# Slot numbers of two or three routed tiles in one set of matmuls, and one query load moved, in an attention, MoE and FFN kernel

## The chip, the cores and the metric

The kernel runs on one core of a Trainium2 chip. The metric is the device time of one execution in microseconds (us); lower is better. Engines are named as in the profile: PE (TensorE matmuls), PEld (its weight loads, which overlap PE), DVE (VectorE), ACT (ScalarE), POOL (GpSimd), SP (the engine that issues most DMAs; SPq is its queue).

## The reference, cut to what matters

```python
# 1. attention, 2 batches x 8 heads, 512 local + 32 global queries, head 64
s_g = scale * q_g @ k_all.T                      # global queries see all keys
s_l = concat([scale * q_l @ k_g.T, where(|i - j| <= 32, scale * q_l @ k_l.T, -1e9)])
out = concat([softmax(s_g) @ v_all, softmax(s_l) @ v_all])
x = out as [1152 tokens, 512]
# 2. top-1 routing to 8 experts with a capacity
expert_idx = argmax(x @ w_gate)
for i in range(N):                               # tokens in order
    e = expert_idx[i]
    if counts[e] < capacity:
        disp[e, counts[e]] = x[i]; pos[i] = counts[e]; counts[e] += 1; keep[i] = True
h = maximum(einsum('ecd,edf->ecf', disp, w1), 0); y = einsum('ecf,efd->ecd', h, w2)
out[i] = gate_w[i] * y[expert_idx[i], pos[i]] if keep[i] else 0
# 3. FFN: x @ w_in, a piecewise activation, @ w_out
```

The change touches the numbers `pos[i]` of part 2, the load of `q_g` in part 1, and matmuls that compute nothing at the kernel's start.

## The kernel before

**Attention** is a loop over 16 steps k = (batch b, half tp of the local queries, pair hp of heads). A unit u = 4 b + hp holds the keys, queries and values of one pair of heads in one batch. Step k issues, in this order on every engine: the exponentials of step k + 1 (`exps`, ACT), the scores of step k + 2 (`scores`: L308 on PE, L313 on DVE), the list `first[k]`, the transposes of step k (`transp`, L333), their copies (`evac_t`, L338 on ACT and L339 on DVE), the product with the values of step k - 1 (`av`, L351 on PE, copy L356 on DVE), and the list `plan[k]`. There is no scheduler: each engine runs its instructions in the order in which the code issues them, and semaphores keep them apart.

**Global queries** are treated in four groups g of two units, by `glob1` (products L367 on PE, maxima L372 to L375 on DVE), `glob1b` (exponentials L383 and L385 on ACT, then L388, L390 and L391 on DVE), `glob2` and `glob3` (L419 on PE, L424 on ACT). They lie in `plan` from steps 0, 3, 5 and 8 on; `glob1` of the last group (g = 3) is in step 8. Its queries, the tile `qgt` for units 6 and 7, are loaded by `load_values(7)`, which is in `plan[6]`, as the last of the DMAs of unit 7. All the loads of this stage (keys and queries `kr` and `qr`, L124 and L125; values `vt`, L130; `qgt`, L133; expert weights `raw`, L205; zeros that fill the routing buffer `xd`, L621) are issued by SP in program order.

**Routing** is done in four parts of tiles of tokens (a tile is 128 tokens, the tile of global tokens 32): (b, lo, hi) = (0, 0, 3), (0, 3, 5), (1, 0, 3) and (1, 3, 5). For each part, `recips` (L507, L508), `logits`, `choose` (up to L536, which writes the one-hot expert of each token, `OH`), `slots` (the running number of each token within its expert, `sidx`), `x_rows` (L487 on PE, L501 on DVE or L498 on ACT) and `scatter` (L566, an indirect DMA that POOL issues). `slots` is in steps 8, 11 and 14, and after the loop for the last part. It makes, tile by tile, a sum of small matmuls in PSUM: the base row of each expert (L547), the counts of all earlier parts (`racc`, L548), the one-hot tiles of the same part that come earlier (L550) and the tokens before each one in its own tile (`tri_b`, L551); so 3, 4 and 5 matmuls for three tiles, 3 and 4 for two. DVE then multiplies with `OH`, reduces to `sidx` and adds to `racc` (L554 to L561).

In steps 5 to 12 a chunk of expert weights is rounded on ACT (`weight_h`, L218) and the rest is taken on POOL (`weight_l`, L230), each at the end of its step and so behind the step's `scatter` on POOL.

After the loop, the last part's rows are brought by a matmul with a matrix of ones (`place`, L739) straight into the first expert's input, and then come the eight experts (L842, L860) and the FFN (L1158, L1198).

**At the start** `keep_warm(WARM_0)` runs nine matmuls of zeros of 512 columns (L629), each with a load of 128 weight columns, ahead of the first `scores`. There are further such bursts around the last `slots`.

Of the kernel before, what the change touches and what calls it, by code (L numbers as in the profile page):

```python
# [8 lines left out]
F32 = mybir.dt.float32  # L9
F32R = mybir.dt.float32r  # L10
BF16 = mybir.dt.bfloat16
# [5 lines left out]
ENG = mybir.EngineType  # L17

P = 128
WARM_0, WARM_1, WARM_2, WARM_3, WARM_4 = 9, 5, 3, 2, 0  # L20
WIN = 224


# [5 lines left out]
def tile_attention_moe_ffn(  # L29
# [23 lines left out]
    nc = tc.nc  # L53
    w_in, w_out = w_in.bitcast(U32), w_out.bitcast(U32)
    B, NHP = qd.shape[0], qd.shape[1]
    SL = qd.shape[3]
    EXT = kd.shape[3]
    SG = qg.shape[3] // 4
# [3 lines left out]
    E, _, F = w1.shape  # L62
# [14 lines left out]
    at = actx.enter_context(tc.tile_pool(name="at", bufs=1))  # L77
# [19 lines left out]
    def ps_a(name):  # L97
        return ps_tile("A", name)
# [4 lines left out]
    def ps_v(name, hold=False):  # L103
        return ps_tile("V", name, hold)
# [7 lines left out]
    KR, QR, VT, QG = {}, {}, {}, {}  # L112

    def load_unit(u, part=None):
        b, hp = divmod(u, NHP)
        if part in (None, 0):
            KR[u] = at.tile([P, EXT], F32, tag="kr", name=f"kr{u}", bufs=NBU)
            QR[u] = at.tile([P, SL], F32, tag="qr", name=f"qr{u}", bufs=NBU)

        for i, (k0, k1, q0, q1) in enumerate(((0, SL // 2 + 96, 0, SL // 2), (SL // 2 + 96, EXT, SL // 2, SL))):  # L120
            if part in (None, i) and (part is not None or i == 0):
                if part is None:
                    k1, q1 = EXT, SL
                nc.sync.dma_start(KR[u][:, k0:k1], kd[b, hp, :, k0:k1])  # L124
                (nc.scalar if u == 0 else nc.sync).dma_start(QR[u][:, q0:q1], qd[b, hp, :, q0:q1])  # L125

    def load_values(u):
        b, hp = divmod(u, NHP)
        VT[u] = at.tile([P, 5, P], F32, tag="vt", name=f"vt{u}", bufs=NBU)
        nc.sync.dma_start(VT[u], vx[b, hp])  # L130
        if hp % 2 == 1:
            QG[u // 2] = at.tile([P, 4 * SG], F32, tag="qgt", name=f"qgt{u}", bufs=4)
            nc.sync.dma_start(QG[u // 2], qg[b, hp // 2])  # L133

    mask_sb = at.tile([P, NLT, WIN], F32, name="mask_sb")
    load_unit(0, 0)
# [4 lines left out]
    zero = const.tile([P, DM], F32, name="zero")  # L141
    nc.gpsimd.memset(zero, 0.0)
    ident = const.tile([P, P], F32, name="ident")
    make_identity(nc, ident)
    load_values(0)
    load_unit(3, 0)
    load_values(1)
    for u in range(NHP):
        load_unit(u, 1)
    nc.sync.dma_start(mask_sb[:, 2:], masks[:, 2:])  # L150
    load_values(2)
    load_values(3)
    wg_sb = const.tile([P, NHP, 32], F32, name="wg_sb")
# [7 lines left out]
    tri_b = const.tile([P, P], BF16, name="tri_b")  # L161
    ones_b = const.tile([P, P], BF16, name="ones_b")
    half = const.tile([P, 1], F32, name="half")
    racc = const.tile([P, E], BF16, name="racc")
    base_b = const.tile([P, E], BF16, name="base_b")
# [131 lines left out]
    def scores(s):  # L297
        b, tp, hp = steps[s]
        u = b * NHP + hp
        SM[s] = at.tile([P, 4, WIN], F32, tag="sm", name=f"sm{s}", bufs=4)  # L300
        NG[s] = at.tile([P, 4], F32, tag="ng", name=f"ng{s}", bufs=3)

        sp = [{1: ps_t, 2: ps_v}.get(s, ps_a)(f"sp{s}_{h}") for h in range(2)]
        for t in range(2):
            i = 2 * tp + t
            for h in range(2):
                hs = slice(D * h, D * h + D)
                nc.tensor.matmul(sp[h][:, t * WIN:(t + 1) * WIN], QR[u][hs, i * P:(i + 1) * P],  # L308
                                 KR[u][hs, i * P:i * P + WIN], start=True, stop=True)
        for h in range(2):  # L310
            for t in range(2):
                c = 2 * t + h
                nc.vector.tensor_tensor_reduce(  # L313
                    out=SM[s][:, c, :], in0=sp[h][:, t * WIN:(t + 1) * WIN], in1=mask_sb[:, 2 * tp + t, :],
                    op0=ALU.add, op1=ALU.min, scale=-scale, scalar=3.0e38, accum_out=NG[s][:, c:c + 1])
# [113 lines left out]
    LG, M8, I8, OH, SC, PL, XR = {}, {}, {}, {}, {}, {}, {}  # L429
# [10 lines left out]
    def tile_rows(i):  # L440
        return SG if i == 0 else P
# [98 lines left out]
    def slots(b, lo, hi):  # L540

        pc = ps_v(f"pc{b}{lo}")
        n = hi - lo
        for i in range(lo, hi):
            o = pc[:, E * (i - lo):E * (i - lo + 1)]
            r = tile_rows(i)
            nc.tensor.matmul(o, ones_b[:1], base_b[:1], start=True, stop=False)  # L547
            nc.tensor.matmul(o, ones_b, racc, start=False, stop=False)  # L548
            for j in range(lo, i):
                nc.tensor.matmul(o, ones_b[:tile_rows(j)], OH[b][:tile_rows(j), j, :], start=False, stop=False)  # L550
            nc.tensor.matmul(o, tri_b[:r], OH[b][:r, i, :], start=False, stop=True)  # L551
        ts = slice(b * NB_ + lo, b * NB_ + hi)
        ex = rt.tile([P, NB_, E], F32, tag="ex", name=f"ex{b}{lo}", bufs=1)
        nc.vector.tensor_tensor(  # L554
            out=ex[:, :n, :], in0=pc[:, :E * n].rearrange("p (i e) -> p i e", e=E), in1=OH[b][:, lo:hi, :],
            op=ALU.mult)
        rs = rt.tile([P, E], F32, tag="rs", name=f"rs{b}{lo}", bufs=1)
        nc.vector.tensor_reduce(out=rs, in_=OH[b][:, lo:hi, :].rearrange("p i e -> p e i"), op=ALU.add, axis=AX.X)
        with nc.allow_low_precision(reason="whole numbers, one of the terms not zero"):
            nc.vector.tensor_reduce(out=sidx[:, ts], in_=ex[:, :n, :], op=ALU.add, axis=AX.X)  # L560
        nc.vector.tensor_tensor(out=racc, in0=racc, in1=rs, op=ALU.add)  # L561
# [61 lines left out]
            nc.sync.dma_start(yd[0:1, :], zero[:1, :])  # L623


    def keep_warm(n):
        warm = ps_a("warm")
        for _ in range(n):
            nc.tensor.matmul(warm, zero.bitcast(BF16)[:, :P], zero.bitcast(BF16)[:, :512], start=True, stop=True)  # L629

    keep_warm(WARM_0)
    scores(0)
    exps(0)
    scores(1)
# [6 lines left out]
    load_values(4)  # L641
    load_unit(5)
    load_values(5)
    wq = [(u, c) for u in range(2) for c in range(4)]
    wn = 0

# [12 lines left out]
    def route(k, b, tp):  # L659

        lo, hi = (0, 3) if tp == 0 else (3, 5)
        i = 2 * tp + 1
        x = [lambda j=j: x_rows(b, j) for j in range(lo, hi)]
        sc = [lambda j=j: scatter(b, j) for j in range(lo, hi)]
        first[k] += [lambda: logits(b, i, 2), lambda: recips(b, i, i + 2)]
        plan[k] += [lambda: logits_t(b, i, 2)]
        if tp == 0:
            first[k].append(lambda: logits(b, 0, 1))
            plan[k].append(lambda: logits_t(b, 0, 1))
        plan[k] += [lambda: choose(b, lo, hi)]  # L670
        first[k + 1] += x[:1]
        plan[k + 1] += [lambda: slots(b, lo, hi)] + x[1:2] + sc[:1]
        plan[k + 2] += x[2:] + sc[1:]
# [42 lines left out]
    for i in (3, 4):  # L716
        x_rows(1, i, (2, 3))
    keep_warm(WARM_1)
    slots(1, 3, NB_)
    late = [XR[1, 3], XR[1, 4]]  # L720
    halves = [[rt.tile([P, DM], F32R, name=f"late{i}{n}") for n in "hl"] for i in range(2)]
# [6 lines left out]
    for (xa, xb), x in zip(halves, late):  # L728
        nc.vector.tensor_tensor(out=xb, in0=x, in1=xa.bitcast(F32), op=ALU.subtract)
    px0 = ps_t("px0")  # L730
    keep_warm(WARM_2)
    parts = [(halves[i][0], place[:, i, :]) for i in range(2)] + [(xt0, ident)]
    parts += [(halves[i][1], place[:, i, :]) for i in range(2)]
# [14 lines left out]
    pc = ps_v("pcnt")  # L748
# [662 lines left out]
```

## Time and profile before

| | |
|---|---|
| runs | 462.73, 465.33, 465.10 us; median 465.1 us |
| the profiled execution | 462.71 us, of which the span from first to last instruction is 460.8 us |
| PE, PEld busy | 442.3 us (96% of the span), 372.1 us (81%) |
| DVE, ACT, POOL busy | 335.2 us (73%), 242.9 us (53%), 95.8 us (21%) |
| instructions | 8110, of them 2875 matmuls |

Each engine's busy share is a mean over stages with different limits: attention with routing ends some 91 us after the span's start, the experts at 254 us, the FFN at the end. What ends the waits within a stage is read from the order of time there, in which each line has its start, its length, the engine, the line of code, and in brackets how long the engine was idle before it and what released it.

### The profile page before, as it was taken

Reading aid. Unit: us, or ns where it says so; the run is one execution under the profiler, and the core shown is the slowest. Engines: PE = TensorE matmul, PEld = TensorE weight load, DVE = VectorE, ACT = ScalarE, POOL = GpSimd, SP = SyncE. Lnnn points to the kernel's source line nnn. Section 1 sums busy time; section 2 is a strip of 40 time slices with the busy share of each in tenths; the row PEclk is TensorE's granted clock in tenths of the full one; section 3 lists DMA queues with packets and bytes.
Section 4 is the critical chain, followed back from the end, with each engine's and each line's share of the span. In section 5 each row is a group of like instructions: output and inputs, shape, how many; then the busy total and the mean of one; then the engine's idle time right before and its main releaser. Section 6 shows DMA issues by size and latency. Waiting matters only on the chain. (4 is left out here: it accounts for less than half of the span.)

```text
span 460.8 us, 8110 instructions
## 1 busy us (share of the span) xinstructions
PE 442.3 (96%) x2875; PEld 372.1 (81%) x2876; DVE 335.2 (73%) x715; ACT 242.9 (53%) x508; POOL 95.8 (21%) x98
## 2 busy tenths in 40 slices
PE   8998989999999999999999899998999999999997
PEld 4876677787577777777777799998999899999996
DVE  4787798674156389936898976787888988878633
ACT  5779666273244478726766675645444344534321
POOL 1105365300000000000001642232133131322321
PEclk9999999999999999999999999999999999999999
DMA  8999554589349169963986340653221410000203
GB/s 273 312 332 366 171 185 134 192 278 395 129 127 316 47 242 389 375 239 123 341 299 243 98 149 0 211 200 93 91 75 64 134 49 1 0 2 0 70 1 127
DMA packets 34595, 79.17 MB, mean 172 GB/s; under 512 B 3761, under 2 KB 8497, under 8 KB 34546
## 3 DMA queue, kind: packets, MB, share of 16 engines
q1 hardware_dynamic: 31698, 70.40, 44.8%
q0 software_dynamic: 1408, 4.46, 2.9%
q10 hardware_dynamic: 1440, 3.67, 2.3%
q8 instruction: 29, 0.48, 0.5%
q14 instruction: 20, 0.16, 0.1%
HBM read 63.77 MB, written 14.75 MB: 170 GB/s over the span
## 5 line engine op out<-in xcount | busy, mean ns | idle before, releaser
L1158 PE MATMUL fh<-oldH,H 128*128 128x256 f32 (+1 forms) x256 | 64.7, 328 | 2.6 <-DVE g L1176 2.1
L230 DVE TENSOR_TENSOR L<-raw,H 128x1024 fp32r<-128x1024 f32 x56 | 66.3, 1217 | 0.9 <-ACT H L218 0.6
L1198 PE MATMUL acc<-oldH,H 128*128 128x256 f32 (+2 forms) x240 | 65.1, 332 | 1.3 <-ACT H L280 0.7
L218 ACT CAST H<-raw 128x1024 fp32r<-128x1024 f32 x57 | 58.0, 1049 | 10.0 <-PEq L895 8.2
L1158 PEld LDWEIGHTS fh<-oldH,H 128*128 128x128 f32 x256 | 44.8, 189 | 6.0 <-DVE g L1176 2.5
L1184 ACT CAST oldH<-g 128x256 fp32r<-128x256 f32 (+2 forms) x36 | 17.9, 496 | 56.8 <-DVE g L1176 56.8
L1198 PE MATMUL acc<-oldH,L 128*128 128x256 f32 (+2 forms) x144 | 47.2, 328 | 0.0
L1198 PEld LDWEIGHTS acc<-oldH,H 128*128 128x128 f32 x240 | 43.3, 189 | 4.0 <-issue 1.0
L1172 DVE SCALAR_TENSOR_TENSOR r<-r 128x256 f32<-128x256 f32 (+2 forms) x48 | 31.2, 650 | 21.0 <-ACT r L1163 21.0
L1185 POOL TENSOR_TENSOR oldH<-g,oldH 128x256 fp32r<-128x256 f32 (+2 forms) x24 | 26.8, 1119 | 73.3 <-ACT oldH L1184 63.5
L1158 PE MATMUL fh<-oldH,L 128*128 128x448 f32 (+1 forms) x128 | 41.6, 325 | 0.0
L599 DVE TENSOR_TENSOR hl<-pt,hh 128x512 fp32r<-128x512 f32 (+1 forms) x24 | 15.7, 653 | 35.6 <-ACT hh L598 35.6
L860 PE MATMUL py<-H,hh 128*128 128x512 f32 (+1 forms) x96 | 38.6, 402 | 0.0
L860 PE MATMUL py<-L,hh 128*128 128x512 f32 (+1 forms) x96 | 37.6, 391 | 0.0
L285 DVE TENSOR_TENSOR L<-co,H 128x512 fp32r<-128x512 f32 x32 | 22.9, 722 | 18.4 <-ACT H L280 18.4
L1163 ACT ACTIVATE r<-fh,half 128x256 f32<-128x256 f32 (+2 forms) x48 | 27.0, 564 | 17.5 <-PE fh L1158 17.1
L845 ACT ACTIVATE hs<-ph 128x512 f32<-128x512 f32 (+1 forms) x24 | 14.4, 598 | 41.2 <-PE ph L842 41.0
L1158 PE MATMUL fh<-oldL,H 128*128 128x384 f32 x128 | 35.2, 339 | 0.2
L931 POOL DMA_INDIRECT yg_own<-yd,idx x2 | 2.3, 1135 | 147.5 <-DVE co L270 147.2
L270 DVE SCALAR_TENSOR_TENSOR co<-raw,ca 128x512 uint32<-128x512 uint32 x32 | 31.5, 992 | 0.9
L324 ACT ACTIVATE sm<-sm,ng 128x224 f32<-128x224 f32 x64 | 30.0, 476 | 3.7 <-DVE ng L313 3.7
L860 PE MATMUL py<-H,hl 128*128 128x512 f32 (+1 forms) x96 | 28.5, 401 | 0.0
(202 smaller groups left out, 1014.8 us busy)
## 6 DMA issues: line engine op xcount, KB each, us to landing
raw<-in_w_dram SPq DMA_DIRECT2D x64, 512.0 KB, 5.7
raw<-in_w_in_dram SPq DMA_DIRECT2D x14, 512.0 KB, 4.9
raw<-in_w_out_dram SPq DMA_DIRECT2D x12, 512.0 KB, 3.7
xd<-zero SPq DMA_DIRECT2D x16, 256.0 KB, 5.9
vt<-in_vx_dram SPq DMA_DIRECT2D x8, 320.0 KB, 4.8
xt<-xd SPq DMA_DIRECT2D x8, 256.0 KB, 6.5
yd<-zero SPq DMA_DIRECT2D x8, 256.0 KB, 3.7
yd<-ys SPq DMA_DIRECT2D x8, 256.0 KB, 5.6
```

What stands on the lines that cost most here:

```text
L218: nc.scalar.copy(dst, src)
L230: eng.tensor_tensor(out=L[:, sl], in0=RAW.pop((u, c)), in1=H[:, sl].bitcast(F32), op=ALU.subtract)
L270: nc.vector.scalar_tensor_tensor(out=o, in0=lo, scalar=29, in1=a, op0=ALU.logical_shift_right, op1=ALU.bitwise_or)
L285: nc.vector.tensor_tensor(out=L[:, sl], in0=CV.pop((g, c)), in1=H[:, sl].bitcast(F32), op=ALU.subtract)
L324: nc.scalar.activation(SM[s][:, c, :], SM[s][:, c, :], AF.Exp, bias=NG[s][:, c:c + 1], scale=-1.0, accum_out=SUM[b][:, i, col:col + 1])
L860: nc.tensor.matmul(py[:rows], h[:, 4 * q + k, :rows], w[:, 4 * q + k, :], start=q == i == 0, stop=q == 1 and i == len(terms) - 1)
L1158: nc.tensor.matmul(ph[:, :n], w[:, k, :], XC[c][i // 2][:, k, :], start=n_ == 0, stop=n_ == len(terms) - 1)
L1163: nc.scalar.activation(RS[f % 2][:, :n], ph[:, :n], AF.Relu, bias=half, scale=0.5)
L1172: nc.vector.scalar_tensor_tensor(out=r[:, :n], in0=r[:, :n], scalar=1.0, in1=r[:, :n], op0=ALU.min, op1=ALU.mult)
L1184: nc.scalar.copy(gh[:, :n], gt[:, :n])
L1185: nc.gpsimd.tensor_tensor(out=gl[:, :n], in0=gt[:, :n], in1=gh[:, :n].bitcast(F32), op=ALU.subtract)
L1198: nc.tensor.matmul(a[:, :n], p[:, ds], q, start=f == 0 and i == 0, stop=f == nfl - 1 and i == 2)
```

## The change

1. `slots` writes the slot numbers of all tiles of a part into one row of PSUM: one matmul each for the base row and for `racc`, with the moving operand repeated over the tiles, one matmul for each earlier tile that adds it to all later tiles at once, and one with `tri_b` for all tiles. Three tiles take 5 matmuls in place of 12, two take 4 in place of 7. The tile of global tokens is now read over all 128 rows.
2. `load_queries` is split off `load_values`, and the queries of group 3 are loaded right behind `load_values(5)`, ahead of the loop, and no longer behind the values of unit 7.
3. The burst at the start has 29 matmuls of 160 columns in place of 9 of 512.

```diff
-WARM_0, WARM_1, WARM_2, WARM_3, WARM_4 = 9, 5, 3, 2, 0
+WARM_0, WARM_1, WARM_2, WARM_3, WARM_4 = 29, 5, 3, 2, 0
...
-        if hp % 2 == 1:
-            QG[u // 2] = at.tile([P, 4 * SG], F32, tag="qgt", name=f"qgt{u}", bufs=4)
-            nc.sync.dma_start(QG[u // 2], qg[b, hp // 2])
+        if hp % 2 == 1 and u // 2 not in QG:
+            load_queries(u // 2)
+
+    def load_queries(g):
+        QG[g] = at.tile([P, 4 * SG], F32, tag="qgt", name=f"qgt{g}", bufs=4)
+        nc.sync.dma_start(QG[g], qg[divmod(2 * g, NHP)[0], 2 * g % NHP // 2])
...
-        for i in range(lo, hi):
-            o = pc[:, E * (i - lo):E * (i - lo + 1)]
-            r = tile_rows(i)
-            nc.tensor.matmul(o, ones_b[:1], base_b[:1], start=True, stop=False)
-            nc.tensor.matmul(o, ones_b, racc, start=False, stop=False)
-            for j in range(lo, i):
-                nc.tensor.matmul(o, ones_b[:tile_rows(j)], OH[b][:tile_rows(j), j, :], start=False, stop=False)
-            nc.tensor.matmul(o, tri_b[:r], OH[b][:r, i, :], start=False, stop=True)
+        o = pc[:, :E * n].rearrange("p (i e) -> p i e", e=E)
+        nc.tensor.matmul(o, ones_b[:1], base_b[:1].unsqueeze(1).to_broadcast([1, n, E]), start=True, stop=False)
+        nc.tensor.matmul(o, ones_b, racc.unsqueeze(1).to_broadcast([P, n, E]), start=False, stop=False)
+
+        for j in range(1, n):
+            nc.tensor.matmul(o[:, j:], ones_b, OH[b][:, lo + j - 1:lo + j, :].to_broadcast([P, n - j, E]),
+                             start=False, stop=False)
+        nc.tensor.matmul(o, tri_b, OH[b][:, lo:hi, :], start=False, stop=True)
...
-    def keep_warm(n):
+    def keep_warm(n, cols=512):
         warm = ps_a("warm")
         for _ in range(n):
-            nc.tensor.matmul(warm, zero.bitcast(BF16)[:, :P], zero.bitcast(BF16)[:, :512], start=True, stop=True)
-
-    keep_warm(WARM_0)
+            nc.tensor.matmul(warm[:, :cols], zero.bitcast(BF16)[:, :P], zero.bitcast(BF16)[:, :cols], start=True,
+                             stop=True)
+
+
+    keep_warm(WARM_0, 160)
...
     load_unit(5)
     load_values(5)
+    load_queries(3)
```

## Rows read from the trace of the kernel before

**Rows 1.** Busy time by stage: stretch, length, busy time of each engine, clock, DMA share.

```profile
76.90:84.70 7.80, 7.74 (x85) 6.77 (x82) 5.73 (x18) 0.59 (x1) 2.84 (x3) 1.00 0.28 101
91.30:254.00 162.70, 159.41 (x755) 120.98 (x756) 109.96 (x166) 93.90 (x145) 3.26 (x4) 1.00 0.71 253
254.00:460.80 206.80, 198.82 (x1180) 187.85 (x1180) 157.31 (x277) 91.36 (x177) 60.90 (x56) 1.00 0.24 76
```

**Rows 2.** PE in order of time, step 8: start, length, work, idle time and releaser.

```profile
42.90 1.03 PE L308 MATMUL sp<-kr,qr 64*128 64x224 f32 x8 [1.88 <-DVE m L532]
...
46.21 1.67 PE L419 MATMUL gpv<-gT,vt 128*64 128x32 f32 x40
...
48.82 1.12 PE L367 MATMUL g<-kr,qgt 64*32 64x288 f32 x16 [0.94 <-DMA qgt<-in_qg_dram]
...
49.87 0.17 PE L547 MATMUL pc<-base_b,ones_b 1*128 1x8 bf16 x1
...
50.94 0.64 PE L487 MATMUL px<-ident,xT 128*128 128x128 f32 x4
```

**Rows 3.** The line that loads keys, 41.0 to 42.0 us (unit 7): issue and landing.

```profile
L124 SPq DMA_DIRECT2D kr<-in_kd_dram x1: 422/422/422, 41.6 to 41.6; - x1
...
DMA to landing us min/median/max: 5.4/5.4/5.4
```

**Rows 4.** The line that loads local queries, 36.0 to 36.2 us (unit 6): issue and landing.

```profile
L125 SPq DMA_DIRECT2D qr<-in_qd_dram x1: 733/733/733, 36.0 to 36.0; - x1
...
DMA to landing us min/median/max: 6.7/6.7/6.7
```

**Rows 5.** SP's queue where the moved load goes (the queries of group 2).

```profile
20.95 0.43 SPq L133 DMA_DIRECT2D qgt<-in_qg_dram  x1
```

**Rows 6.** Busy time, clock, DMA share and GB/s ahead of step 8.

```profile
33.00:43.00 10.00, 8.04 (x120) 6.35 (x118) 7.45 (x31) 9.90 (x32) 5.30 (x3) 1.00 1.02 377
```

**Rows 7.** DVE and POOL in order of time, steps 8 and 9.

```profile
49.56 0.46 DVE L372 TENSOR_REDUCE gs<-g 128x1 f32<-128x288 f32 x1 [2.57 <-PE g L367]
...
51.12 0.18 DVE L554 TENSOR_TENSOR ex<-pc,oh 128x24 f32<-128x24 f32 x1 [0.32 <-PE pc L551]
...
52.40 1.11 POOL L566 DMA_INDIRECT xd<-xr,sidx  x1 [7.62 <-DVE xr L501]
...
53.55 2.37 POOL L230 TENSOR_TENSOR L<-raw,H 128x1024 fp32r<-128x1024 f32 x1
...
54.98 0.97 DVE L388 SCALAR_TENSOR_TENSOR gs<-gs 128x1 f32<-128x1 f32 x1
```

**Rows 8.** DVE and POOL in order of time, steps 10 to 13.

```profile
58.45 2.53 DVE L507 TENSOR_SCALAR ssum<-ssum 128x16 f32<-128x16 f32 x1
...
58.57 4.78 POOL L230 TENSOR_TENSOR L<-raw,H 128x1024 fp32r<-128x1024 f32 x2
...
67.47 0.99 POOL L566 DMA_INDIRECT xd<-xr,sidx  x1 [4.11 <-DVE racc L561]
...
72.05 2.39 POOL L230 TENSOR_TENSOR L<-raw,H 128x1024 fp32r<-128x1024 f32 x1
```

**Rows 9.** PE and DVE in order of time, the slots of step 11.

```profile
66.19 0.17 PE L547 MATMUL pc<-base_b,ones_b 1*128 1x8 bf16 x1
...
66.81 0.17 DVE L554 TENSOR_TENSOR ex<-pc,oh 128x16 f32<-128x16 f32 x1 [0.25 <-PE pc L551]
```

**Rows 10.** PE in order of time, the slots of step 14.

```profile
76.97 0.17 PE L547 MATMUL pc<-base_b,ones_b 1*128 1x8 bf16 x1
...
78.16 0.64 PE L487 MATMUL px<-ident,xT 128*128 128x128 f32 x4
```

**Rows 11.** DVE in order of time, the last slots.

```profile
86.89 0.16 DVE L554 TENSOR_TENSOR ex<-pc,oh 128x16 f32<-128x16 f32 x1
```

**Rows 12.** PE in order of time, the start.

```profile
1.31 3.88 PE L629 MATMUL warm<-zero 128*128 128x512 bf16 x9 [1.31 <-POOL zero L142]
...
5.12 1.91 PE L308 MATMUL sp<-kr,qr 64*128 64x224 f32 x16
```

## The prediction

> **What bounds the kernel now.** I read the stages first [rows 1]: in the experts and in the FFN PE is busy for 159.41 of 162.70 us and 198.82 of 206.80 us. None of the change's instructions run there. Time that the change gains or loses ahead of the experts should therefore arrive at the end almost unchanged, as their start and the weight loads that follow freed buffers move with it. The question is only what the change does to the first 91 us, and there I read the order of time, engine by engine, around `slots`, around the moved load and at the start. The reader is to see three kinds of bound in turn. Up to step 8 the bound is the DMA queue: its engines are fully booked from 33 to 43 us [rows 6], and PE, which idles for 1.88 us ahead of the scores at 42.90, starts just after unit 6's queries land at 36.0 + 6.7 = 42.7 us [rows 2, 4]. (The row names a DVE instruction as releaser; by its own line that had long been needed for nothing in `scores`, whose operands are `qr` and `kr`.) From there to the slots of step 8 PE itself is the chain, except for one hole: it ends `glob3` at 46.21 + 1.67 = 47.88 and starts `glob1` of group 3 at 48.82, held for 0.94 us by its queries [rows 2]. From step 9 to 13 the chain goes through DVE and POOL: POOL takes up scatters when DVE's rows are ready, then rounds weights, and DVE instructions wait for the end of that [rows 7, 8]. Last, from 76.90 to 84.70 it is PE again, busy for 7.74 of 7.80 us [rows 1].
>
> **The moved load: what it gives.** With `qgt` there since some 20 us earlier, the 0.94 us go, if nothing else is late. Next in line are the keys of unit 7: 41.6 + 5.4 = 47.0 us, 0.9 us before PE is through with `glob3` [rows 2, 3]. So the whole 0.94 us is free to go. DVE has 2.57 us idle ahead of the maxima of group 3 [rows 7], so it follows PE.
>
> **The moved load: what it costs.** It is 128 rows of 128 floats, 65.5 KB, on SP's queue at about 21.4 us, behind the load of group 2 [rows 5]; it is moved past the zero fills of `xd`, the first expert weights and the loads of units 6 and 7, which are all behind it now. In a queue that moves 377 GB/s at full share [rows 6] it is worth 65.5 / 377 = 0.17 us; as an issue on SP it is 0.43 us [rows 5]. The landing at 42.7 us that PE waits for [rows 4] moves by that: nothing at best (the DMA engines may have a gap that takes it), 0.43 us at worst. I take 0.2 us, near the byte price, because a queue that is full is paced by bytes and not by issues. At its old place it stood behind everything that matters, so its going there gives nothing more.
>
> **The slots, step 8.** Twelve matmuls take PE from 49.87 to the next work at 50.94, 1.07 us, 0.089 us each [rows 2]; they are small (8 columns, 0.17 us from start to end) and come one after the other, so I count them by pace. Five cost 0.45 us: 0.62 us saved. Their moving operand grows to 24 columns at most; eight `sp` matmuls of 224 columns each pass in 1.03 us [rows 2], so 16 more are put at nothing, with 0.02 us as the other end. On PE the two gains make 0.94 - 0.2 + 0.62 = 1.36 us. The chain then passes to DVE. The maxima start 0.74 us earlier; DVE works on from 49.56 to 50.80 and waited 0.32 us more for `pc` [rows 7]. That wait is all that the shorter `slots` gives it: 0.74 + 0.32 = 1.06 us. POOL's scatter at 52.40 waits for DVE and its rounding at 53.55 comes next; DVE's L388, 0.97 us for one column, ends just when that rounding ends (53.55 + 2.37 = 55.92, 54.98 + 0.97 = 55.95) [rows 7]. So the end of this stall moves with POOL, by **1.06 us**, and PE's other 0.3 us are lost in it.
>
> **The slots, step 11.** Seven matmuls become four: 3 x 0.089 = 0.27 us. DVE waited 0.25 us for them [rows 9], and the scatter at 67.47 waited for DVE; two roundings and a scatter later POOL ends its last rounding at 72.05 + 2.39 = 74.44, and DVE stands still until then [rows 8]. I take 0.2 us, with 0 and 0.25 as ends: ACT, which must first deliver the rounded half, may be the later one.
>
> **The slots, step 14.** Twelve become five again, in a stretch in which PE is the chain: 78.16 - 76.97 = 1.19 us [rows 10], of which some goes by in waiting for `OH`, so 0.5 us, with 0.25 us (DVE's own path keeps about half) and 0.62 us as ends.
>
> **The last slots** give nothing: DVE comes to `ex` at 86.89 with no idle time before it [rows 11], so it was its own earlier work that it was waiting for. What hides the saving is `x_rows` on DVE; without that cover it would be 0.2 us more gain.
>
> **The burst at the start** has 4640 columns in place of 4608. Nine matmuls take 3.88 us, 0.43 us each [rows 12], which is 512 columns at 1.2 GHz, though the clock is given as full. At that pace 160 columns take 0.133 us and 29 matmuls 3.87 us. That counts the weight loads as hidden, as they are in the burst of before. The nearest row of short pairs is `glob3`: 40 loads of 64 columns with their matmuls in 1.67 us, 0.042 us a pair [rows 2]; twice the columns at half the clock make at most 0.167 us, and 29 of those 4.84 us. So the first scores, at 5.12 [rows 12], start between now and 1.0 us later. Either way the end does not see it: PE stands for 1.88 us at 42.90 waiting for a DMA [rows 2] that SP issues without regard to it. Taken at nothing; a start 1.88 us late or more would cost the excess.
>
> **Sum.** 1.06 + 0.2 + 0.5 = 1.76 us off. The ends: 0.94 - 0.43 + 0 + 0 + 0.25 = 0.8 us and 0.94 + 0.32 + 0.25 + 0.62 = 2.1 us. Against the profiled execution that is 462.71 - 1.8 = 460.9 us (1.9 us of it lie outside the span). The median of the runs shown is 2.4 us above that execution, for a reason that this trace does not show, and the time to come is a median too: 465.1 - 1.8 = **463.3 us**.
>
> **Rivals.**
>
> *The gain is taken back on POOL and DVE.* The stalls end when a rounding on POOL ends, and a rounding needs its half from ACT and its raw weights from the DMA. If one of those is late where POOL was, step 9 to 13 end where they did, and only step 14's 0.5 us remain: 464.6 us. For it: POOL works through its roundings in order, and two stand back to back at 58.57 [rows 8]. Against it: the scatter at 52.40 ends a POOL idle time of 7.62 us and was released by DVE [rows 7], not by ACT.
>
> *A stall changes sides.* At 58.45 `recips` loses by about 0.1 us against a rounding that starts at 58.57, and takes 2.53 us [rows 8]. A shift of a tenth may turn this, and `recips` would be through at once. But the one-hot of the same part follows on DVE, has both inputs in SBUF too, and would meet the same pair of roundings, which runs to 58.57 + 4.78 = 63.35; I price it at 0.3 us more gain (an estimate between nothing and the 2.53 us): 463.0 us. The Trainium skill has a rule here ("SBUF — State Buffer", section "Who interferes with whom"): DVE and GpSimd share a port pair, and whichever instruction issues first keeps it until it ends. By the recorded starts DVE was first at 58.45 and still waited, so the rows do not bear the rule out to a tenth of a microsecond; by it the gain here would be the one just priced.
>
> *The start is late: slower.* If the narrow burst leaves PE at 1.2 GHz, the scores and transposes that follow run at half pace. PE starts on 1.91 us of scores at 5.12 [rows 12] and attention follows at once, so each microsecond that the low clock lasts beyond that costs up to one more. The 1.88 us at 42.90 absorb the first of it and the gain above another 1.8, so it turns into a loss once the low clock lasts past about 9 us; until 13 us it would be 8 - 1.9 - 1.8 = 4.3 us slower, 469.4 us. For it: the gaps between loads and matmuls are new. Against it: as many columns in as much time.
>
> *It doesn't do what it says*: the unit's other loads are as late as the queries were, pushed by 0.43 us, and the slots were never waited for on the chain: 465.1 us, no change.
>
> **How the numbers follow.** Forecast 0.62, POOL takes it back 0.15, stall turned 0.08, late start 0.07, no effect 0.08. The range takes in the sum's ends, 463.0 and 464.3, the rival at 465.1, and the runs' own spread around the median, -2.4 and +0.2: below, a median as low as the profiled execution with most of the gain, 462.71 - 2.1, makes 460.6; above, no gain and a run at the top, with up to 0.7 us of the late start, 466.0. So 460.5 to 466.0. The runs of before spread over 2.6 us, and I count 1% (4.65 us) as what a measurement can tell. Faster than that needs a gain twice my upper end, or part of it with a favourable spread: 0.08. Slower needs the late start in full: 0.04. The rest, 0.88, is within 1%.
>
> **What would show it.** In the profile of the changed kernel: `glob1` of group 3 following `glob3` with no idle time, at 48.0 to 48.3; unit 6's scores at 43.1; the slots of step 8 in 0.45 us; DVE's L388 still stalled, ending near 54.9; the last rounding ending near 73.2; the first expert matmul at about 89.5, where it is 91.3 now [rows 1]; the first scores between 5.1 and 6.1. I would be wrong if PE waits for unit 7's keys where it waited for queries, if the stalls of DVE come at other places, if the first scores run at half pace, or if the experts take up the gain waiting for weights.

## The result, and the profile after

The changed kernel is slower: 467.71 us median (465.81 to 471.33) against 464.64 us (462.73 to 465.78) in ten runs each. The ratio, taken over the runs and not from the two medians, is 1.0077, with a 95% interval of 1.0052 to 1.0103. The forecast was 463.3 us, and its range ended at 466.0.

The profiled execution of the changed kernel took 467.27 us (span 465.4 us, mean granted clock 0.993). I began with the stages, in the columns of [rows 1]: the last piece of PE-bound attention, the experts, the FFN.

```profile
80.60:88.90 8.30, 8.26 (x94) 7.03 (x93) 6.92 (x29) 1.52 (x4) 2.85 (x3) 1.00 0.35 127
95.60:258.50 162.90, 159.63 (x756) 121.09 (x756) 109.97 (x166) 94.00 (x145) 3.34 (x4) 1.00 0.71 253
258.50:465.40 206.90, 198.91 (x1180) 187.78 (x1179) 156.92 (x276) 91.29 (x176) 61.41 (x56) 1.00 0.24 76
```

Experts and FFN are as long as before to 0.2 us and 0.1 us. The whole loss, 95.6 - 91.3 = 4.3 us, is there before the first expert matmul. So I went through PE in order of time and set each landmark against the one of before [rows 2, 9, 10].

```profile
44.15 1.03 PE L311 MATMUL sp<-kr,qr 64*128 64x224 f32 x8 [1.55 <-DMA qr<-in_qd_dram]
...
47.45 1.67 PE L422 MATMUL gpv<-gT,vt 128*64 128x32 f32 x40
49.05 0.68 PE L370 MATMUL g<-kr,qgt 64*32 64x288 f32 x4
49.96 1.11 PE L370 MATMUL g<-kr,qgt 64*32 64x288 f32 x12 [0.23 <-DMA kr<-in_kd_dram]
51.00 0.18 PE L548 MATMUL pc<-base_b,ones_b 1*128 1x24 bf16 x1
...
51.22 0.64 PE L490 MATMUL px<-ident,xT 128*128 128x128 f32 x4
...
65.19 1.11 PE L490 MATMUL px<-ident,xT 128*128 128x128 f32 x4 [4.28 <-DVE xT L359]
...
71.48 0.18 PE L548 MATMUL pc<-base_b,ones_b 1*128 1x16 bf16 x1
...
71.68 0.64 PE L490 MATMUL px<-ident,xT 128*128 128x128 f32 x4
...
82.04 0.18 PE L548 MATMUL pc<-base_b,ones_b 1*128 1x24 bf16 x1
...
82.46 0.64 PE L490 MATMUL px<-ident,xT 128*128 128x128 f32 x4
```

Two rows of before answer to the ones at 65.19 and 71.68 and were not shown yet: the same transposes at the start of step 11, and the work behind the slots of that step.

```profile
62.20 0.65 PE L487 MATMUL px<-ident,xT 128*128 128x128 f32 x4 [1.57 <-DVE xT L356]
...
66.63 0.64 PE L487 MATMUL px<-ident,xT 128*128 128x128 f32 x4
```

Read as a ledger of after minus before, it runs like this.

| landmark on PE | before | after | late by |
|---|---|---|---|
| unit 6's scores | 42.90 | 44.15 | 1.25 |
| slots of step 8, first matmul | 49.87 | 51.00 | 1.13 |
| work behind them | 50.94 | 51.22 | 0.28 |
| transposes at the start of step 11 | 62.20 | 65.19 | 2.99 |
| slots of step 11, first matmul | 66.19 | 71.48 | 5.29 |
| work behind them | 66.63 | 71.68 | 5.05 |
| slots of step 14, first matmul | 76.97 | 82.04 | 5.07 |
| work behind them | 78.16 | 82.46 | 4.30 |

The slots do what was claimed: PE saves 1.13 - 0.28 = 0.85 us, 0.24 us and 0.77 us in them. But between 51.22 and 71.48 PE loses 5.01 us, in two pieces: 2.71 us ahead of the transposes of step 11, and 2.30 us in the work that follows. The first piece is explained on DVE and POOL, the second by the clock. DVE, POOL and ACT of the changed kernel in order of time, against [rows 7, 8]:

```profile
50.68 0.46 DVE L375 TENSOR_REDUCE gs<-g 128x1 f32<-128x288 f32 x1 [2.12 <-PE g L370]
...
51.84 0.17 DVE L557 TENSOR_TENSOR ex<-pc,oh 128x24 f32<-128x24 f32 x1
...
55.26 1.40 DVE L391 SCALAR_TENSOR_TENSOR gs<-gs 128x1 f32<-128x1 f32 x1
...
59.16 4.82 DVE L510 TENSOR_SCALAR ssum<-ssum 128x16 f32<-128x16 f32 x1
...
59.28 4.67 POOL L233 TENSOR_TENSOR L<-raw,H 128x1024 fp32r<-128x1024 f32 x2
...
60.14 1.05 ACT L221 CAST H<-raw 128x1024 fp32r<-128x1024 f32 x1
```

`recips` (L510, 16 columns) stands for 4.82 us in place of 2.53: it now waits through both of POOL's roundings, where in the kernel before it got in between them. (There the two roundings take 4.78 us together, here 4.67 us: the 0.11 us less are the gap.) Everything behind it on DVE waits as well, the copy of `xT` (L359) among it, for which PE idles 4.28 us in place of 1.57.

Busy time and granted clock of the changed kernel where that idle time lies (the clock is the third number from the end, just ahead of the DMA share):

```profile
60.00:64.00 4.00, 0.91 (x8) 0.56 (x8) 3.99 (x1) 3.06 (x10) 3.95 (x2) 0.91 0.52 185
64.00:68.00 4.00, 2.81 (x14) 2.41 (x14) 3.88 (x22) 0.59 (x1) 0.00 (x0) 0.50 0.58 190
68.00:72.00 4.00, 4.00 (x64) 3.82 (x64) 1.75 (x7) 0.40 (x2) 0.00 (x0) 0.74 0.00 0
```

After the idle time the granted clock is 0.50, the 1.2 GHz level, and the transposes of 0.65 us take 1.11 us. From their start to the slots of step 11 PE needs 71.48 - 65.19 = 6.29 us for what took 66.19 - 62.20 = 3.99 us before. That is the second piece, 2.30 us.

At the start, the narrow burst and the first scores, against [rows 12]:

```profile
1.31 4.05 PE L632 MATMUL warm<-zero 128*128 128x160 bf16 x29 [1.31 <-POOL zero L145]
5.29 2.88 PE L311 MATMUL sp<-kr,qr 64*128 64x224 f32 x24
```

The scores start 0.17 us later and at the pace of before, 0.12 us a matmul (2.88 us for 24 against 1.91 us for 16); in this execution the rival of a late start is out.

### The profile page after: what moved, and what is told of

It reads as the page before. It is cut to its first block, busy times and chain, and to the rows that moved or that the text cites. A ratio compares the mean times of both kernels' runs of the same rounds, so it can differ in the third digit from the quotient of the medians.

```text
span 465.4 us, 8112 instructions
## 1 busy us (share of the span) xinstructions
PE 443.7 (95%) x2876; PEld 374.9 (81%) x2876; DVE 337.4 (72%) x715; ACT 242.7 (52%) x508; POOL 96.2 (21%) x98
```

## The experiments

The theory that I took into them (A): PE's lead over DVE and POOL brings ACT's rounded half `H` early enough for POOL's second rounding to follow the first without a gap, `recips` stands through both, and the hole on PE then costs the clock. The rivals: the moved load does it, by pushing other loads (B), or the narrow burst does (C).

**One part at a time.** Three kernels with a single part of the change, each made from the kernel before.

```diff
# e1_slots: only the new body of slots
# e2_load: only
+    load_queries(3)        # behind load_values(5), with load_queries split off
# e3_burst: only
-    keep_warm(WARM_0)      # 9 of 512 columns
+    keep_warm(WARM_0, 160) # 29 of 160 columns
```

> The kernel before with the new slots alone. Theory A (the shorter slots let PE, and with it ACT's rounded half, gain on DVE and POOL, so that two roundings on POOL follow each other without a gap and recips in step 10 stands through both): the stall of recips is about 4.8 us, the granted clock falls below 1.00, and the time is 2 to 5 us above before. Theory B (the moved load makes the DMA queue late): no loss here, recips at 2.5 us, clock 1.00, 1 us faster than before or the same. Theory C (the burst): as B.

> The kernel before with the moved load alone. Theory A: PE and DVE gain alike from the load, so the stall of recips stays at 2.5 us, the clock at 1.00, and the time is 0 to 1 us below before. Theory B: the first expert weights land 1 to 2 us later and the time is 2 to 5 us above before, with a clock below 1.00. Theory C: as before.

> The kernel before with the burst of 29 narrow matmuls alone. Theories A and B: within 0.5 us of before, clock 1.00, recips at 2.5 us. Theory C: 2 to 5 us above before, and a clock below 1.00.

The slots alone: 1.0016 (0.9988 to 1.0045). The load alone: **0.9929** (0.9907 to 0.9951), 462.06 us, the best part by far. The burst alone: 1.0033 (1.0013 to 1.0053). In time these three do not decide: the interval of the slots alone holds 1, short of the 2 to 5 us that A expected, and the burst alone is slower, which A did not expect and C nearly did (467.08 us against 465.10 us, where C had 2 to 5 us). The traces say more. That of the slots alone has the long `recips` and, behind it, the low clock:

```profile
57.55 4.82 DVE L507 TENSOR_SCALAR ssum<-ssum 128x16 f32<-128x16 f32 x1
...
62.00:64.00 2.00, 0.42 (x2) 0.43 (x3) 1.93 (x7) 0.00 (x0) 0.33 (x1) 0.57 0.63 190
64.00:66.00 2.00, 2.00 (x12) 1.94 (x10) 1.93 (x15) 0.36 (x1) 0.00 (x0) 0.50 0.66 234
```

With the load alone and with the burst alone `recips` takes 2.53 us. So the stall belongs to the slots (A), not to the load (B) nor the burst (C). The trace of the burst alone shows one reason why the load gains so much more than its forecast. PE in order of time in step 8, then the windows there:

```profile
49.92 1.12 PE L367 MATMUL g<-kr,qgt 64*32 64x288 f32 x16 [2.11 <-DMA qgt<-in_qg_dram]
...
48.00:52.00 4.00, 2.08 (x26) 1.39 (x26) 1.17 (x4) 2.88 (x10) 0.00 (x0) 0.88 1.00 375
52.00:56.00 4.00, 4.00 (x20) 3.03 (x21) 2.02 (x10) 0.00 (x0) 2.39 (x2) 0.50 0.12 36
```

That kernel still has the late `qgt`. In this execution the hole is 2.11 us and not the 0.94 of [rows 2], and the clock falls to 0.50 behind it.

**Parts left out.** The changed kernel with the old slots, and with the old burst.

```diff
# e6_load_burst: the old body of slots
# e7_load_slots:
-    keep_warm(WARM_0, 160)
+    keep_warm(WARM_0)      # 9 of 512 columns
```

> The changed kernel with the slots of before (moved load and narrow burst stay). Theory A: as the moved load alone, 461.5 to 463 us, clock 1.00 in most runs, recips at 2.5 us. If the narrow burst itself lowers the clock later (it measured 2 us above before by itself): 463.5 to 465 us.

> The changed kernel with the burst of before (moved load and new slots stay). Theory A: as the changed kernel, 466 to 469 us, recips at 4.8 us. If the burst has a share in the loss: 464 to 466 us.

Without the new slots 0.9983 (0.9959 to 1.0006), `recips` 2.52 us; without the narrow burst 1.0066 (1.0038 to 1.0094), `recips` 4.81 us. The long `recips` and the loss stay with the slots and go with them. The burst changes little beside them (1.0066 against 1.0077), but beside the load alone it costs 0.5% (0.9983 against 0.9929), and alone 0.33%. No row of these traces shows where; that stays open.

**A gap made on POOL.** A memset of 16 columns on POOL between the two roundings, to let DVE in.

```diff
+    pause = at.tile([P, 16], F32, name="pause")
...
+            if k == 10:
+                nc.gpsimd.memset(pause, 0.0)
             weight_l(*wq[c], nc.gpsimd)
```

> The changed kernel with one small memset on POOL ahead of the rounding of step 10, so that POOL lets go of what it holds between the two roundings. Theory A: recips gets in at the end of the first rounding, 2.5 us in place of 4.8, PE's idle time behind it falls from 4.3 to about 2 us, the clock stays at 1.00, and the time falls by 3 to 6 us, to 462 to 464.5 us. Theories B and C: no change, 467 us. If the memset is too short or if what is held is not let go by it, recips stays at 4.8 us and A is neither borne out nor refuted.

A miss: 1.0066 (1.0035 to 1.0098). The memset runs and DVE is not let in.

```profile
56.84 4.88 DVE L510 TENSOR_SCALAR ssum<-ssum 128x16 f32<-128x16 f32 x1
...
56.96 2.38 POOL L233 TENSOR_TENSOR L<-raw,H 128x1024 fp32r<-128x1024 f32 x1
59.25 0.14 POOL L705 MEMSET pause<- 128x16 f32 x1
59.32 2.36 POOL L233 TENSOR_TENSOR L<-raw,H 128x1024 fp32r<-128x1024 f32 x1
```

An instruction between is no gap as long as POOL has the next one ready. What would be one is POOL having to wait, and the next kernel makes it wait.

**The rounded half made late.** The second rounding's two instructions are issued a step later, behind its exponentials, with the slots as in the change.

```diff
+        if k == 11:
+            weight_h(*wq[5], nc.scalar)
+            weight_l(*wq[5], nc.gpsimd)
...
-        if 5 <= k < 13:
+        if 5 <= k < 13 and k != 10:
```

> The changed kernel with the rounding of step 10, its half on ACT and its rest on POOL, issued in step 11 behind the exponentials, so that the half is ready only after the rounding of step 9 has ended on POOL. Theory A (DVE gets in only if POOL has nothing ready when a rounding ends): recips ends with the first rounding, 2.5 us in place of 4.8, PE idles there for about 2 us, clock 1.00 around it, and the time falls to 462 to 465 us. If recips is held by something else than the second rounding: 4.8 us and 467 us as before.

**0.9953** (0.9919 to 0.9987), 462.69 us: from 1.0077, with all three parts of the change still in.

```profile
57.74 2.52 DVE L510 TENSOR_SCALAR ssum<-ssum 128x16 f32<-128x16 f32 x1
...
57.84 2.37 POOL L233 TENSOR_TENSOR L<-raw,H 128x1024 fp32r<-128x1024 f32 x1
...
61.69 2.36 POOL L233 TENSOR_TENSOR L<-raw,H 128x1024 fp32r<-128x1024 f32 x1 [1.48 <-ACT H L221]
```

POOL now waits 1.48 us for ACT's half, and `recips` is through after the first rounding. The rule can be checked over all kernels that have `recips` in its place, by how long after the start of the first rounding ACT starts its CAST for the second:

| kernel | first rounding starts | CAST starts | CAST later by | `recips` takes |
|---|---|---|---|---|
| e7_load_slots | 56.32 | 57.16 | 0.84 | 4.81 |
| e8_fill (below) | 56.57 | 57.42 | 0.85 | 4.82 |
| the change | 59.28 | 60.14 | 0.86 | 4.82 |
| e4_gap | 56.96 | 57.91 | 0.95 | 4.88 |
| e1_slots | 57.66 | 58.62 | 0.96 | 4.82 |
| e10_before_fill (below) | 60.39 | 61.67 | 1.28 | 2.52 |
| before | 58.57 | 59.86 | 1.29 | 2.53 |
| e2_load | 60.11 | 61.40 | 1.29 | 2.53 |
| e6_load_burst | 58.71 | 60.00 | 1.29 | 2.52 |
| e3_burst | 61.68 | 63.69 | 2.01 | 2.53 |
| e9_late_half | 57.84 | 60.59 | 2.75 | 2.52 |

The five with the new slots and the old order of the roundings stand at 0.96 or less, the others at 1.28 or more, and nothing lies between. The CAST takes 1.05 us and the rounding 2.38, so at 1.29 the half is there 0.04 us ahead of the rounding's end, and that is already late enough for DVE to get in. The kernel before stood at most 1.29 - 0.96 = 0.33 us inside the good side, and the new slots moved it by 0.43 us.

What the stall costs can be read from the traces in a stretch that leaves out the arrival of the loads: from PE's first matmul in the slots of step 8 to the first expert matmul. (Some of these kernels are described below.)

| kernels | slots | `recips` of step 10 | stretch, us |
|---|---|---|---|
| before, e2_load, e6_load_burst, e10_before_fill | old | 2.52 to 2.53 us | 41.4 to 41.7 |
| e3_burst, where the clock fell at the stretch's start | old | 2.53 us | 43.7 |
| the change, e1_slots, e4_gap, e7_load_slots | new | 4.81 to 4.88 us | 44.0 to 45.5 |
| e8_fill, hole filled | new | 4.82 us | 42.3 |
| e9_late_half | new | 2.52 us | 40.9 |
| e5_recips_early, e11_rec_fill, e12_both_early | new | moved to step 8 | 39.4 to 39.9 |

With `recips` as long as before, the new slots shorten the stretch by 0.5 to 0.8 us; with `recips` moved away as well it is 1.5 to 2.3 us shorter; with the long `recips` it is 2.3 to 4.1 us longer. Behind the first expert matmul these traces take 369.5 to 371.0 us, except for e11_rec_fill and e12_both_early (below) and for e7_load_slots with 372.9 us: of the 4.1 us by which that execution's span is longer than the one of before, 3.4 us lie there, and their cause is open.

**`recips` taken out of the pair's way.** The sums that it needs are there by step 8, so it goes to that step's list. (The expectation names step 11 by the slots; `recips` stands in the list of step 10.)

```diff
-        first[k] += [lambda: logits(b, i, 2), lambda: recips(b, i, i + 2)]
+        first[k] += [lambda: logits(b, i, 2)]
+        first[8 if k == 10 else k].append(lambda: recips(b, i, i + 2))
```

> The changed kernel with the recips of tiles 3 and 4 of batch 0 issued in step 8, when POOL rounds nothing, in place of step 11. Theory A (what the slots cost is recips standing through both roundings, which holds DVE, so PE, so the clock): no DVE instruction of 4.8 us, PE's idle time there below 2 us, clock 1.00 in most runs, 459 to 463 us. If A is wrong about recips and any DVE instruction in the way of PE would do, the one-hot of the same tiles takes over the wait and the time stays at 466 to 468 us.

**0.9935** (0.9914 to 0.9957), 461.5 us.

```profile
46.75 0.16 DVE L510 TENSOR_SCALAR ssum<-ssum 128x16 f32<-128x16 f32 x1
...
61.57 2.38 DVE L539 TENSOR_TENSOR oh<-iota_sb,i 128x16 bf16<-128x16 f32 x1
...
60.75 0.65 PE L490 MATMUL px<-ident,xT 128*128 128x128 f32 x4
```

`recips` takes 0.16 us where POOL is idle. The one-hot (L539) meets the second rounding in its place, but the copies that PE needs are ahead of it on DVE: PE comes to the transposes of step 11 without idle time.

**The clock's share.** The hole is left and filled with 18 matmuls of zeros on PE, ahead of the transposes that wait.

```diff
+        if k == 11:
+            fill = ps_t("fill")
+            for _ in range(18):
+                nc.tensor.matmul(fill, zero.bitcast(BF16)[:, :P], zero.bitcast(BF16)[:, :512], start=True, stop=True)
```

> The changed kernel with 18 matmuls of zeros of 512 columns (some 3.9 us at full clock) on PE between the scores of step 13 and the row turn in step 11, where PE idles. It takes the idle time and leaves recips standing. If the fallen clock is a cost of its own: recips still at 4.8 us, but a clock of 1.00 from 62 to 72 us, and 2 to 3 us less than the changed kernel, 464.5 to 466 us. If the clock costs nothing: no change or slower.

1.0008 (0.9978 to 1.0039), 463.72 us. `recips` still takes 4.82 us (the table); what is gone is the clock's fall.

```profile
58.12 4.06 PE L693 MATMUL fill<-zero 128*128 128x512 bf16 x18
62.49 0.66 PE L490 MATMUL px<-ident,xT 128*128 128x128 f32 x4 [0.32 <-DVE xT L359]
...
64.00:68.00 4.00, 4.00 (x73) 3.57 (x72) 3.94 (x17) 1.67 (x4) 0.46 (x1) 1.00 0.09 32
```

So of the change's loss some 1.0077 - 1.0008 = 0.7%, 3.2 us, is clock; with both intervals this is uncertain by some 0.4%. The ledger has 2.30 us for it, and the stretches above 44.0 - 42.3 = 1.7 us to 45.5 - 42.3 = 3.2 us.

The kernel before, with nine such matmuls ahead of `glob1` of group 3 in step 8, asks whether the load gains by the clock alone:

```diff
+        if g == 3:
+            fill = ps_t("fill")
+            for _ in range(9):
+                nc.tensor.matmul(fill, zero.bitcast(BF16)[:, :P], zero.bitcast(BF16)[:, :512], start=True, stop=True)
```

> The kernel before with nine matmuls of zeros (1.9 us at full clock) on PE ahead of the global products of group 3, where it waits for their queries. If the 3 us that the moved load gains by itself are mostly the clock that falls in this hole: clock 1.00 in most runs and 462 to 463.5 us without moving the load. If they are the wait itself: 464 to 465.5 us, as before or slower.

1.0001 (0.9970 to 1.0032). The time is in the branch in which the load gains by the wait itself, but this is inconclusive: five of its ten runs have a granted clock of 0.999 or more, against 7 of 31 of the kernel before beside them, and the fill takes PE time of its own (2.12 us, where the hole of [rows 2] is 0.94 us). The gain of the load is not had by it.

**Both cures together: two misses.** e5_recips_early with five zero matmuls in step 8, where PE waits for unit 6's queries; and the same with the `recips` of step 13 moved to step 12 as well.

```diff
+        if k == 8:
+            fill = ps_t("fill")
+            for _ in range(5):
+                nc.tensor.matmul(fill, zero.bitcast(BF16)[:, :P], zero.bitcast(BF16)[:, :512], start=True, stop=True)
# e12_both_early, in place of the line of e5_recips_early:
+        first[{10: 8, 13: 12}.get(k, k)].append(lambda: recips(b, i, i + 2))
```

> The changed kernel with recips of tiles 3 and 4 of batch 0 in step 8 and five matmuls of zeros (1.1 us) ahead of the scores issued in step 8, where PE waits for the queries of unit 6. Theory: the half of the runs of recips-early that had a clock of 0.996 lost it in this hole; now 1.00 in nearly all, 460 to 461.5 us median. If the hole was not its cause: 461.5 us and the same mix of clocks.

> As the kernel with recips early and five matmuls of zeros, and the recips of tiles 1 and 2 of batch 1 in step 12 in place of 13, when POOL is between two roundings. Theory A: its stall of 1.9 to 2.4 us goes, and as PE waited some 0.7 us behind it, 459 to 461 us. If it only moves on to the next DVE instruction with two inputs in SBUF: no change against the kernel without it.

1.0031 (1.0003 to 1.0059) and 1.0043 (1.0015 to 1.0070). In the first the experts start at 88.9 us, 2.4 us ahead of the kernel before; the loss is behind that. PE in order of time, and the window:

```profile
237.66 0.77 PE L853 MATMUL ph<-H,x0h 128*128 128x512 f32 x1 [3.99 <-PEq L906]
...
235.00:240.00 5.00, 2.34 (x6) 1.91 (x7) 4.01 (x9) 0.00 (x0) 0.00 (x0) 0.75 0.79 263
```

PE waits 3.99 us for its own sequencer at a branch between two experts (L906), and the clock falls behind it. In the changed kernel and the one before no such wait there is longer than 0.4 us; in e12_both_early it is 4.1 us. Why the branch takes so long in these two is open: e8_fill, with 18 added matmuls, does not have it. So whether the two cures add up was not measured.

## Why the prediction was wrong

**The step that failed** is the slots of step 8: "So the end of this stall moves with POOL, by **1.06 us**, and PE's other 0.3 us are lost in it." PE's lead over DVE and POOL was not lost. It went to ACT, which follows PE, and ACT's half for POOL's second rounding came 0.43 us earlier against POOL. On DVE and POOL the step was read rightly: L391 (L388 in the kernel before) ends with POOL's rounding, 55.26 + 1.40 = 56.66 us against 54.26 + 2.37 = 56.63 us. The forecast treated the pair of roundings [rows 8] as one block that moves as a whole; it had a gap, and `recips` lived on it. The row had said so: `recips`, begun at 58.45, ended at 60.98, in the middle of a pair that ran from 58.57 to 63.35.

**The rival "a stall changes sides"** named the place and the instruction, and had the sign wrong. It moved the start of `recips` against the pair and priced 0.3 us of gain; what moved was the second rounding against the first, at +2.3 us for `recips` and +2.7 us for PE. The Trainium skill ("SBUF — State Buffer", section "Who interferes with whom") has the port pair of DVE and GpSimd as a lock that is held for a whole instruction. The traces agree that DVE gets in only at an instruction's end: `recips` ends at 59.16 + 4.82 = 63.98, the second rounding at 59.28 + 4.67 = 63.95. Which of the two asked first they do not show: DVE's record starts at 59.16, ahead of POOL's 59.28, but the record of the instruction ahead of it on DVE (L316) runs until 59.24. In all eleven kernels of the table of CASTs `recips` waits out the first rounding; what differs is whether the second follows at once.

**The rival "the gain is taken back on POOL and DVE"** looked at the right input, ACT's half, for the opposite reason: it feared a half that comes late, and the loss came from one that was early.

**The clock was left out.** The prediction followed a profiled execution at clock 1.00 and said that the 2.4 us to the median had a reason that the trace did not show. The runs suggest it: of 88 runs of the kernel before beside the experiments, the 14 with a mean granted clock of 0.999 or more have a median of 463.6 us, the 32 under 0.995 one of 465.7 us. Where in those runs the clock fell is not recorded. Traces of other kernels show two places ahead of `recips`: the hole for `qgt` in e3_burst, and the wait for unit 6's queries in e2_load, e5_recips_early and e6_load_burst. In e2_load:

```profile
43.83 1.87 PE L311 MATMUL sp<-kr,qr 64*128 64x224 f32 x8 [2.81 <-DMA qr<-in_qd_dram]
...
44.00:46.00 2.00, 2.00 (x10) 1.36 (x11) 1.11 (x2) 0.20 (x2) 0.77 (x1) 0.50 1.00 332
```

The scores that took 1.03 us in [rows 2] take 1.87 us here. In e5_recips_early the wait is 1.54 us, and the clock is 0.60 from 44 to 46 us; in the kernel before it was 1.88 us, and the clock stayed at 1.00. So the length of one wait alone does not tell. A hole of PE was priced at its own length throughout, and the one ahead of step 11's transposes cost 2.3 us more.

**The moved load** was right as a mechanism and mis-sized. Forecast was 0.94 - 0.2 = 0.74 us; alone it gave 0.71% of 465 us, 3.3 us. The hole that it closes is longer in some executions (2.11 us in e3_burst) and has a price in clock. Six of the seven runs of e2_load have a clock of 1.000 (the seventh is the one of the trace above); none of the ten of e3_burst or of e1_slots, nor of the 27 of the kernel before beside them, is above 0.996. Next in line were unit 7's keys, as said: `glob1` starts at 49.05 behind `glob3`, and waits 0.23 us for them in the middle. The cost of up to 0.43 us at unit 6's queries can't be told apart: the scores that need them are 1.25 us late in this execution, but start at 41.69 in e4_gap and 42.32 in e8_fill, which issue the same instructions as the change up to there, and so ahead of 42.90 in the kernel before. The first row of the ledger is a difference between executions more than one of the change.

**The other terms.** Slots of step 8 on PE 0.85 us (forecast 0.62), of step 11 0.24 us (0.2), of step 14 0.77 us (0.5, above its end of 0.62); the last slots `ex` at 91.19 without idle time, as said. These gains are in the ledger. Where DVE's place between the roundings holds, in e9_late_half, the time is 462.69 us, near the forecast; that is in part luck, as the load alone gave 3.3 us, of which the forecast had 0.74. The burst, taken at nothing, cost 0.33% by itself (1.5 us, e3_burst), and the cause of that is open.

## What to carry to other kernels

Before shortening a step, look on the neighbouring engines for a short instruction that takes far longer than its size (here 16 columns in 2.53 us): it is living on a gap between two long ones, and whoever brings the second one's input earlier closes that gap. Give a hole on PE a second price, the work behind it at half the clock: in each of the four kernels in which it was left open, the hole of 4.3 us cost that too, and waits of 1.4 to 2.8 us did in some executions (e2_load, e3_burst, e5_recips_early, e6_load_burst) and not in others (1.88 us in the kernel before). And take the median's distance from a profiled execution as something to be explained before the sum is set against it. Of this change the moved load alone (462.06 us), or all of it with `recips` moved to step 8 (461.5 us), beats both kernels; their intervals do not tell the two apart.

## What the runs showed of the hardware

- In these kernels `recips`, a DVE instruction that waits for POOL, is let in only where POOL's next instruction is not ready in time: an input that comes 0.04 us ahead of the running one's end is late enough (1.29 us in the table), while a memset of 0.14 us between the two does not help (4.88 us).
- A hole of 4.28 us on PE was followed by a granted clock of 0.50, and work of 3.99 us took 6.29 us; with zero matmuls in the hole (e8_fill) the clock behind it was 1.00.
- A wait of PE of 2.81 us for a load (e2_load) was followed by a clock of 0.50, and one of 2.11 us too (e3_burst); one of 1.88 us in the kernel before was not.
- A branch between two experts held PE for 3.99 us in e11_rec_fill, against 0.4 us at most in e5_recips_early, from which it differs by five matmuls far ahead of the branch.
